# First two blocks of a fused attention and gated-projection kernel: token-partition loads of q and k, transposes on TensorE, and one explicit order of first steps

## The chip, the cores and the metric

The kernel runs on one core of one Trainium2 chip. The metric is device time in microseconds (us); lower is better. Five engines work beside each other and meet only at semaphores: PE (TensorE, matrix products and transposes by products), PEld (its weight loads), DVE (VectorE), ACT (ScalarE) and POOL (GpSimd). SP issues nearly all DMA transfers, in its program order. Each engine also works in its program order.

## The reference, cut to what matters

```
scores = (q_c @ k_c^T) / sqrt(64)            # chunks of 64 tokens, 8 batches, 8 heads, 576 tokens, head size 64
attn   = softmax(scores);  x = attn @ v_c    # x reshaped to (4608 tokens, 512)
y      = (sigmoid(x @ w_gate) * (x @ w_val)) @ w_out         # 512 -> 1536 -> 512
out    = act(y @ w2_in) @ w2_out                             # 512 -> 2048 -> 512
```

The weights w_gate, w_val, w_out, w2_in and w2_out are 64-bit floats and everything else is 32-bit. The change touches only the attention of the first two blocks and the first products with w_gate and w_val.

## The kernel before, in words

**Phases.** Phase one goes through 9 blocks of 512 tokens; for each it makes the attention output x and from it the gated product g, which goes to DRAM. Three later phases multiply by w_out, w2_in and w2_out. Only phase one changes.

**Slots.** A block of phase one has 24 slots, one for each 128 columns of w_gate (even slots) and w_val (odd slots), keys 0 to 23. A slot is one call of `proj`: 12 matmuls of 128x128 by 128x512, three (`three`, lines 482 to 484) for each of four 128-row parts kt of x, since each operand is split in a high and a low part. ACT takes the sigmoid of the gate (line 917) and DVE multiplies (line 920). Part kt of x comes from head pair p = kt of the attention.

**Attention.** The attention of a block runs as four head pairs p = 0 to 3, in steps with letters: t (q and k to head-dimension-on-partitions), s (scores on PE, line 336), m (row maximum and subtraction, DVE), e (exp, ACT, line 353), n (row sums and reciprocal, DVE), w (scaling, POOL, line 366), p (transposes of the scores on PE, line 372), c (copy out of PSUM, ACT, line 375), o (product with v on PE, line 384), x (high part, ACT, line 393) and l (low part, DVE). In block 0 they run before the first slot. The attention of block b + 1 is spread over the slots of block b.

**Three layouts of q and k** in `load` and `t`. V: 16 DMAs for each pair, 32 of 128-byte pieces at a time, then two DVE transposes of 32x32 blocks (line 317). M: 2 DMAs with 1 KB pieces, then plain matmuls against an identity (line 325) and an ACT copy (line 326). T: 4 DMAs with 256-byte pieces on the SBUF side, then four PE transposes (line 322) for q, four for k, each with an ACT copy (line 326). Block 0 takes M, V, M, T for its pairs; all later blocks take V. `swap` is an arrangement of the two heads' halves that V loads use from block 1 on.

**Weights of phase one.** `w_load` brings 512 KB of one key on SP's queue. `w_low` and `w_bits` (lines 113, 119 on DVE, 123 on ACT) and `w_split` (127 on DVE, 136 on ACT, 137 on POOL) turn the 64-bit words into a high and a low 32-bit part. This is needed once, during block 0.

**What sets the order.** The text LOADS gives the order of the first DMAs on SP: a digit loads q and k of that pair, a letter v, w the next key. The text ORDER gives the steps of block 0, where s, n, p and o each stand for a run of steps (sme, nw, pc, oxl) and c for pieces of weight conversion, f for filling matmuls. Everything else goes through `at(slot, priority, function)`: `emit(slot)` gives out the entries of a slot, by fraction and then priority, ahead of that slot's products. In `later_block`, `starts` are the slots at which pairs begin and `when` the offsets of the steps; q and k of a pair are loaded near the start of the pair two before. The constant NW = 4 says that key i is split at slot i - 4; its first conversion is at slot i - 5 and its load at slot i - 9.

**PSUM banks** have tags b0 to b7. In block 0 the transposes use b0, b2, b4 in turn; the scores b1, b3; the gate and value products b0, b1 and b2, b3; block 1 uses b4, b5 for scores, b6 for transposed scores, b6 and b7 for o.

```
kv_["ident"] = cp.tile([P, P], F32, name="ident")
...
begun = [-6.5, -6]
later_block(1, [5 * p for p in range(KT)], (0, 1, 1.5, 2, 3, 3, 5, 5, 6, 6.5, 7))
...
go = proj(("g", f), b, f"b{f % 2}")
```

Of the kernel before, what the change touches and what calls it, by code (L numbers as in the profile page):

```python
# [8 lines left out]
F32 = mybir.dt.float32  # L9
# [9 lines left out]

LOADS = "0w12wwa3bwcdww"
ORDER = (
    "t0 c1 t1 s0 t2 c1 n0 s1 c1 p0 c1 n1 s2 "
    "t3 n2 o0 p1 s3 o1 n3 p2 f2 c1 o2 p3 c1 c1 o3"
)


# [1 line left out]
def kernel(  # L30
# [201 lines left out]
    class Whole:  # L232
# [14 lines left out]

        def swap(self, p):

            return self.b != REST and self.how[p] == "V"  # L250

        def load(self, p):
            t = self.alloc("qk")
            how = self.how[p]
            if how == "V":

                t = t.rearrange("p i (t r) -> p i t r", r=32)
            elif how == "T":

                t = t.rearrange("p i (j h d) -> p i j h d", h=2, d=D)  # L260
            else:
                t = t.rearrange("p i (h j d) -> p i h j d", h=2, d=D)
            for i, src in enumerate((q, k)):
                if self.b == REST:
                    for g in range(4):
                        h, j = divmod(g, 2)
                        for c in range(RS // 32):
                            nc.sync.dma_start(
                                out=t[32 * g:32 * g + 32, i, c::RS // 32],
                                in_=src[:, 2 * p + h, BS + 32 * c:BS + 32 * c + 32, 32 * j:32 * j + 32].rearrange(  # L270
                                    "b i r -> i b r"
                                ),
                            )
                else:
                    rows = src[batch(self.b), 2 * p:2 * p + 2, :BS]
                    if how == "M":
                        nc.sync.dma_start(
                            out=t[:, i].rearrange("i h j d -> i h (j d)"),
                            in_=rows.rearrange("h (i j) d -> i h (j d)", j=NC),
                        )  # L280
                    elif how == "T":
                        for h in range(2):
                            nc.sync.dma_start(
                                out=t[:, i, :, h], in_=rows[h].rearrange("(i j) d -> i j d", j=NC)
                            )
                    else:
                        n = 2 if self.swap(p) else 1
                        step = BS // n
                        for u in range(n):
                            for g in range(4):  # L290
                                h, j = divmod(g, 2)
                                part = rows[h ^ u, u * step:(u + 1) * step, 32 * j:32 * j + 32]
                                nc.sync.dma_start(  # L293
                                    out=t[32 * g:32 * g + 32, i, u * step // 32:(u + 1) * step // 32],
                                    in_=part.rearrange("(t i) r -> i t r", i=32),
                                )
            self.qk[p] = t
# [14 lines left out]
        def t(self, p):  # L312
            qk, how, ident = self.qk[p], self.how[p], kv_["ident"]
            self.T[p] = t = self.alloc("qkT")
            for i in range(2):
                if how == "V":
                    nc.vector.transpose(out=t[:, i].rearrange("p (t i) -> p t i", i=32), in_=qk[:, i])
                    continue
                b = self.bank(0, [P, NC, P], "T")
                for j in range(NC):  # L320
                    if how == "T":
                        nc.tensor.transpose(b[:, j], qk[:, i, j].rearrange("p h d -> p (h d)"), ident)
                    else:
                        for h, hs in enumerate(heads):
                            nc.tensor.matmul(b[hs, j], lhsT=qk[:, i, h, j], rhs=ident, start=True, stop=True)
                nc.scalar.activation(t[:, i].rearrange("e (i j) -> e j i", j=NC), b, AF.Copy)

        def s(self, p):
            t = self.T[p]
# [75 lines left out]
    def first_block():  # L405
        ft = ps.tile([P, BS], F32, tag="b5", name="fill")

        def fill(n):
            for _ in range(n):
                nc.tensor.matmul(ft, lhsT=z[:, :P], rhs=z, start=True, stop=True)  # L410

        pieces = []
        for i in range(NW + 1):
            pieces.append((w_low, keys[i]))
            pieces.append((w_bits, keys[i]))
            if i:
                pieces.append((w_split, keys[i - 1]))
        nl = [0]

        def wl(n):  # L420
            for _ in range(n):
                w_load(keys[nl[0]])
                nl[0] += 1

        def conv(n):
            while n and pieces:
                fn, key = pieces.pop(0)
                fn(key)
                if fn is w_split and nl[0] < NW + 5:
                    wl(1)  # L430
                n -= fn is not w_low

        z = pool["sg"].tile([P, BS], F32R, tag="sg", name="z", bufs=4)
        nc.vector.memset(f32(z), 0.0)
        kv_["ident"] = cp.tile([P, P], F32, name="ident")
        make_identity(nc, kv_["ident"])
        a = Whole(
            0, [["b0", "b2", "b4"], "b1", "b3", "b6", "b7", "b5"],
            lambda nm: wp.tile([P, 2, BS], F32, tag="w", name=nm), "MVMT",
        )  # L440
        for c in LOADS:
            if c == "w":
                wl(1)
            elif c in "0123":
                a.load(int(c))
            else:
                a.v_load("abcd".index(c))
        for c in ORDER.split():
            if c[0] == "f":
                fill(int(c[1:]))  # L450
            elif c[0] == "c":
                conv(int(c[1:]))
            else:
                for fn in {"t": "t", "s": "sme", "n": "nw", "p": "pc", "o": "oxl"}[c[0]]:
                    getattr(a, fn)(int(c[1:]))
        conv(99)
        assert nl[0] == NW + 5, nl

    def block_load(a, p):
        a.load(p)  # L460

    def later_block(b, starts, when):

        bufs = {"qk": 3, "qkT": 1, "sp": 2, "vd": 2}

        def alloc(nm):
            cols = BS // 2 if nm == "vd" else BS
            return pool["u"].tile([P, 2, cols], F32, tag=nm, name=nm, bufs=bufs[nm])

        a = Whole(b, [None, "b4", "b5", "b6", "b6", "b7"], alloc, "V" * KT)  # L470
        for p, s0 in enumerate(starts):
            at(begun[-2] + 0.5, 5, a.load, p)
            begun.append(s0)
            at(s0 + 0.5, 5, a.v_load, p)
            for fn, dt in zip("tsmenwpcoxl", when):
                at(s0 + dt, {"s": 0, "p": 0, "o": 0, "m": 1, "e": 1, "c": 1, "x": 1}.get(fn, 3), getattr(a, fn), p)


    def three(o, pairs, start=True, open_=False):
        for i, (ah, al, bh, bl) in enumerate(pairs):  # L480
            first, last = start and i == 0, i == len(pairs) - 1
            nc.tensor.matmul(o, lhsT=ah, rhs=bh, start=first, stop=False, skip_group_check=open_)  # L482
            nc.tensor.matmul(o, lhsT=ah, rhs=bl, start=False, stop=False, skip_group_check=open_)  # L483
            nc.tensor.matmul(o, lhsT=al, rhs=bh, start=False, stop=last, skip_group_check=open_)  # L484

    def proj(key, b, tag):
        w = W[key]
        o = ps.tile([P, BS], F32, tag=tag, name="pr")
        kts = [slice(kt * P, (kt + 1) * P) for kt in range(KT)]
        three(o, [(w[:, 0, ks], w[:, 1, ks], X[b, kt][:, 0], X[b, kt][:, 1]) for kt, ks in enumerate(kts)])  # L490
        return o

# [308 lines left out]
        dst = gR if b == REST else gT[i // (B // 2)][i % (B // 2)]  # L803
        nc.sync.dma_start(out=dst[f * P:(f + 1) * P, :], in_=sg)

    begun = [-6.5, -6]
    later_block(1, [5 * p for p in range(KT)], (0, 1, 1.5, 2, 3, 3, 5, 5, 6, 6.5, 7))
    for b in range(2, NB):
        later_block(
            b, [NS * (b - 1) + 6 * p - 6 for p in range(KT)], (0, 2, 3, 4, 5, 5.5, 7, 7, 8, 9, 10)  # L810
        )

    NW = 4
    for i, key in enumerate(keys):
        if i >= NW + 5:
            at(i - NW - 5, 2.5, w_load, key)
        if i > NW:
            at(i - NW - 1, 6, w_low, key)
            at(i - NW - 1, 6, w_bits, key)
        if i >= NW:  # L820
            at(i - NW, 5.5, w_split, key)
    slot = 26
# [69 lines left out]
    with tc.manual_schedule():  # L892
# [18 lines left out]
        for b in range(NB):  # L911
            for f in range(F1):
                slot = NS * b + 2 * f
                emit(slot)
                go = proj(("g", f), b, f"b{f % 2}")
                sg = pool["sg"].tile([P, BS], F32, tag="sg", name="sg", bufs=4)
                nc.scalar.activation(sg, go, AF.Sigmoid)  # L917
                emit(slot + 1)
                vo = proj(("v", f), b, f"b{2 + f % 2}")
                nc.vector.tensor_tensor(out=sg, in0=vo, in1=sg, op=ALU.mult)  # L920
                at(slot + 2, 7, g_store, b, f, sg)
        emit(NS * NB)
# [42 lines left out]
```

## Time and profile before

| | before |
|---|---|
| median of 3 runs | 1678.91 us |
| lowest and highest run | 1675.12, 1679.11 us |
| the profiled execution's own time | 1678.13 us |
| its span in the trace | 1676.2 us |
| PE busy in the span | 98% |

The span runs from the first to the last profiled instruction; the execution's time is 1.93 us longer than the span. All times of rows below are counted from the start of the span.

### The profile page before, as it was taken

The page shows a single profiled execution, that of the slowest core. Times are in us where ns is not written, and L with a number is a line of the kernel's source. Part 1 is how long each engine was busy: PE and PEld are TensorE (multiplying, and loading weights), DVE is VectorE, ACT ScalarE, POOL GpSimd, SP SyncE. Part 2 cuts the span into 40 slices and gives each one's busy share as a digit, 9 for nine tenths or more (in the row PEclk, how much of TensorE's full clock was granted, in tenths as well). Part 3 has the DMA queues.
Part 4 walks back from the last instruction along what each step waited for, and adds up shares of the span by engine and source line. Part 5 has one row for each costly group of instructions (what it writes and reads, how often), then busy time and mean ns, then how long its engine had stood idle before and what let it go on. Part 6 is the DMA issues. An engine that isn't in the chain of part 4 may idle for free.

```text
span 1676.2 us, 29838 instructions
## 1 busy us (share of the span) xinstructions
PE 1640.7 (98%) x10658; PEld 1514.1 (90%) x10658; DVE 1153.0 (69%) x1841; ACT 851.1 (51%) x1558; POOL 723.3 (43%) x666
## 2 busy tenths in 40 slices
PE   5899999999999999999999999999999999999999
PEld 4678888887888888899999999999999999999998
DVE  5874455554555541287777777888787899889887
ACT  4663455444544541255555565555554555555553
POOL 2442444443444340155555564444350465545544
PEclk7999999999999999999999999999999999999999
DMA  7676777777787776535744763323427944554462
GB/s 197 158 196 170 207 197 219 224 227 211 212 243 221 191 259 241 212 120 135 229 151 151 252 229 132 151 113 143 151 114 296 354 138 113 168 151 104 124 189 39
DMA packets 408613, 307.14 MB, mean 183 GB/s; under 512 B 284688, under 2 KB 330768, under 8 KB 408464
## 3 DMA queue, kind: packets, MB, share of 16 engines
q1 hardware_dynamic: 405264, 304.84, 59.1%
q8 instruction: 84, 1.38, 0.3%
q10 hardware_dynamic: 3200, 0.39, 0.1%
q14 instruction: 65, 0.53, 0.1%
HBM read 179.83 MB, written 125.30 MB: 182 GB/s over the span
## 4 chain that ended last, share of the span: by engine, by line
PE 87%; DVE 4%; SPq 4%; DMA 3%; issue 1%; ACT 1%; POOL 0%; DVEq 0%; ACTq 0%; POOLq 0%
PE P L483 18%; PE P L484 18%; PE P L482 18%; PE pr L482 10%; PE pr L484 10%; PE pr L483 10%; SPq L293 2%; DMA raw<-in_moe_w_gate_dram 1%; DVE z L515 1%; PE O L384 1%; PE S L336 1%; PE PT L372 1%; SPq L310 1%; DVE z L526 1%; DMA vd<-in_v_dram 1%
## 5 line engine op out<-in xcount | busy, mean ns | idle before, releaser
L483 PE MATMUL P<-z,w 128*128 128x384 f32 x1344 | 450.4, 335 | 1.6 <-POOL z L526 0.8
L482 PE MATMUL P<-z,w 128*128 128x384 f32 x1344 | 449.0, 334 | 0.0
L484 PE MATMUL P<-z,w 128*128 128x384 f32 x1344 | 449.0, 334 | 0.0
L526 POOL TENSOR_TENSOR z<-z 128x384 fp32r<-128x384 f32 x256 | 291.2, 1149 | 361.2 <-ACT z L519 355.1
L482 PE MATMUL pr<-x,w 128*128 128x512 f32 x864 | 345.6, 400 | 0.0
L484 PE MATMUL pr<-x,w 128*128 128x512 f32 x864 | 339.4, 393 | 0.0
L483 PE MATMUL pr<-x,w 128*128 128x512 f32 x864 | 338.8, 392 | 0.0
L519 ACT ACTIVATE z<-z 128x384 fp32r<-128x384 f32 x420 | 211.4, 522 | 165.4 <-DVE z L515 73.5
L920 DVE TENSOR_TENSOR sg<-pr,sg 128x512 f32<-128x512 f32 x108 | 74.5, 690 | 289.4 <-PE pr L484 120.1
L483 PEld LDWEIGHTS P<-z,w 128*128 128x128 f32 x1344 | 252.3, 188 | 4.7 <-POOL z L526 2.6
L484 PEld LDWEIGHTS P<-z,w 128*128 128x128 f32 x1344 | 252.3, 188 | 0.0
L482 PEld LDWEIGHTS P<-z,w 128*128 128x128 f32 x1344 | 252.3, 188 | 0.0
L526 POOL TENSOR_TENSOR op<-in,op 128x384 fp32r<-128x384 f32 x126 | 142.4, 1135 | 196.7 <-ACT op L519 195.7
L484 PEld LDWEIGHTS pr<-x,w 128*128 128x128 f32 x864 | 163.4, 189 | 35.2
L482 PEld LDWEIGHTS pr<-x,w 128*128 128x128 f32 x864 | 163.5, 189 | 34.6
L483 PEld LDWEIGHTS pr<-x,w 128*128 128x128 f32 x864 | 163.7, 189 | 32.6
L519 ACT ACTIVATE op<-in 128x384 fp32r<-128x384 f32 x252 | 128.5, 524 | 111.3 <-DVE in L515 54.2
L515 DVE TENSOR_TENSOR z<-z 128x384 f32<-128x384 f32 x198 | 179.4, 933 | 4.0 <-POOL z L526 4.0
L917 ACT ACTIVATE sg<-pr 128x512 f32<-128x512 f32 x108 | 64.5, 597 | 223.4 <-PE pr L484 217.8
L484 PE MATMUL P<-op,w 128*128 128x384 f32 x504 | 168.3, 334 | 0.0
L482 PE MATMUL P<-op,w 128*128 128x384 f32 x504 | 168.3, 334 | 0.0
L483 PE MATMUL P<-op,w 128*128 128x384 f32 x504 | 168.3, 334 | 0.0
(64 smaller groups left out, 2186.5 us busy)
## 6 DMA issues: line engine op xcount, KB each, us to landing
uT<-ua SPq DMA_DIRECT2D x96, 384.0 KB, 2.3
z<-uT SPq DMA_DIRECT2D x96, 384.0 KB, 6.0
gT<-sg SPq DMA_DIRECT2D x96, 256.0 KB, 4.6
in<-gT SPq DMA_DIRECT2D x48, 384.0 KB, 4.2
raw<-in_moe_w_out_dram SPq DMA_DIRECT2D x28, 512.0 KB, 5.7
w<-swi SPq DMA_DIRECT2D x28, 512.0 KB, 5.6
w<-swp SPq DMA_DIRECT2D x28, 512.0 KB, 7.2
swi<-st SPq DMA_DIRECT2D x24, 512.0 KB, 5.0
```

The lines of the kernel that those rows point to most:

```text
L293: nc.sync.dma_start(out=t[32 * g:32 * g + 32, i, u * step // 32:(u + 1) * step // 32], in_=part.rearrange("(t i) r -> i t r", i=32),)
L310: nc.sync.dma_start(out=t[:, :, hs], in_=rows.rearrange("(g k) d -> k g d", k=P))
L336: nc.tensor.matmul(banks[h ^ u][hs, c], lhsT=t[rows, 0, ts], rhs=t[rows, 1, ts], start=True, stop=True)
L372: nc.tensor.transpose(b[:, cs], self.SP[p][:, 0, cs], kv_["ident"])
L482: nc.tensor.matmul(o, lhsT=ah, rhs=bh, start=first, stop=False, skip_group_check=open_)
L483: nc.tensor.matmul(o, lhsT=ah, rhs=bl, start=False, stop=False, skip_group_check=open_)
L484: nc.tensor.matmul(o, lhsT=al, rhs=bh, start=False, stop=last, skip_group_check=open_)
L515: (eng or nc.vector).tensor_tensor(out=op_src(p, key), in0=x, in1=y, op=ALU.subtract)
L519: nc.scalar.activation(o[:, 0], op_src(p, key), AF.Copy)
L526: eng.tensor_tensor(out=o[:, 1], in0=op_src(p, key), in1=f32(o[:, 0]), op=ALU.subtract)
L917: nc.scalar.activation(sg, go, AF.Sigmoid)
L920: nc.vector.tensor_tensor(out=sg, in0=vo, in1=sg, op=ALU.mult)
```

## The change

The first block's pairs take the layouts M, M, T, T. The second block's pairs take S, V, S, S, where S is T with the `swap` arrangement (8 DMAs for a pair; two DVE transposes are replaced by eight PE transposes and two ACT copies). T and S put token j * 128 + i on partition i, so that each DRAM piece is 256 bytes, and the ACT copy needs no rearrangement. LOADS and ORDER are new; ORDER names every step by its own letter, with A for the first conversion of a key, B for its split, L for a weight load and k for one part (three matmuls) of a product. `proj` is cut in parts (`proj_part`), so that the value product's parts 0 and 1 and the gate product's part 0 run before the last pairs are done. The filling matmuls go. Key i is now split at slot i - 2, its first conversion is at slot i - 3 and its load at slot i - 8. The starts and offsets of block 1 are new.

```
-LOADS = "0w12wwa3bwcdww"
+LAYOUT = "MMTT"
+LOADS = "10www23wabcd"
 ORDER = (
-    "t0 c1 t1 s0 t2 c1 n0 s1 c1 p0 c1 n1 s2 "
-    "t3 n2 o0 p1 s3 o1 n3 p2 f2 c1 o2 p3 c1 c1 o3"
+    "t1 t0 A0 A1 s0 A2 B0 t2 s1 m0 e0 t3 n0 w0 p0 m1 e1 c0 s2 B1 n1 w1 m2 o0 L L s3 x0 p1 "
+    "l0 e2 k01 c1 n2 o1 m3 x1 e3 w2 p2 l1 c2 L n3 w3 k11 o2 x2 k00 l2 p3 c3 o3 L x3 A3 l3 "
 )
...
-                    elif how == "T":
-                        for h in range(2):
-                            nc.sync.dma_start(
-                                out=t[:, i, :, h], in_=rows[h].rearrange("(i j) d -> i j d", j=NC)
-                            )
+                    elif how in "TS":
+                        n = 2 if self.swap(p) else 1
+                        for u in range(n):
+                            js = slice(u * NC // n, (u + 1) * NC // n)
+                            for h in range(2):
+                                nc.sync.dma_start(
+                                    out=t[:, i, js, h],
+                                    in_=rows[h ^ u].rearrange("(j i) d -> i j d", i=P)[:, js],
+                                )
...
-            0, [["b0", "b2", "b4"], "b1", "b3", "b6", "b7", "b5"],
-            lambda nm: wp.tile([P, 2, BS], F32, tag="w", name=nm), "MVMT",
+            0, [["b1", "b3"], "b4", "b5", "b6", "b6", "b7"],
+            lambda nm: wp.tile([P, 2, BS], F32, tag="w", name=nm), LAYOUT,
...
-        a = Whole(b, [None, "b4", "b5", "b6", "b6", "b7"], alloc, "V" * KT)
+        a = Whole(b, [["b4", "b5"], "b4", "b5", "b6", "b6", "b7"], alloc, how)
...
+    def proj_part(key, b, kt):
+        w, ks = W[key], slice(kt * P, (kt + 1) * P)
...
+        args = w[:, 0, ks], w[:, 1, ks], X[b, kt][:, 0], X[b, kt][:, 1]
+        three(o[0], [args], start=kt == 0, stop=kt == KT - 1, open_=True)
+
+    def proj(key, b):
+        for kt in range(parts.get((key, b), (None, 0))[1], KT):
+            proj_part(key, b, kt)
+        return parts.pop((key, b))[0]
...
-    begun = [-6.5, -6]
-    later_block(1, [5 * p for p in range(KT)], (0, 1, 1.5, 2, 3, 3, 5, 5, 6, 6.5, 7))
+    begun = [-5.5, -2.5]
+    later_block(1, [3.0, 8, 13.0, 17.0], (-1.5, 1.5, 2.0, 2.0, 2.5, 3.0, 5.0, 5, 6.0, 7.0, 7.0), "SVSS")
...
-    NW = 4
+    NA, NW, NL = 4, 2, 8
     for i, key in enumerate(keys):
-        if i >= NW + 5:
-            at(i - NW - 5, 2.5, w_load, key)
-        if i > NW:
-            at(i - NW - 1, 6, w_low, key)
-            at(i - NW - 1, 6, w_bits, key)
+        if i >= NL:
+            at(i - NL, 2.5, w_load, key)
+        if i >= NA:
+            at(i - NW - 1, 7, w_low, key)
+            at(i - NW - 1, 7, w_bits, key)
         if i >= NW:
             at(i - NW, 5.5, w_split, key)
```

## Rows read from the trace of the kernel before

**Rows 1.** The profile page's first part: busy time of each engine.
```profile
PE 1640.7 (98%) x10658; PEld 1514.1 (90%) x10658; DVE 1153.0 (69%) x1841; ACT 851.1 (51%) x1558; POOL 723.3 (43%) x666
```

**Rows 2.** Busy time by stretch: stretch, length, engines' busy time (count), clock, DMA share, GB/s.
```profile
0.00:39.10 39.10, 22.11 (x346) 18.53 (x346) 20.36 (x50) 17.59 (x28) 7.84 (x12) 0.72 0.80 207
39.10:51.90 12.80, 10.62 (x61) 8.04 (x58) 8.47 (x16) 6.76 (x12) 4.43 (x4) 0.67 0.39 63
51.90:89.10 37.20, 32.57 (x256) 26.08 (x256) 32.32 (x56) 23.36 (x36) 16.98 (x13) 0.95 0.77 210
89.10:129.20 40.10, 37.01 (x282) 29.74 (x281) 29.25 (x58) 25.39 (x39) 15.45 (x12) 1.00 0.67 171
129.20:201.70 72.50, 72.50 (x561) 59.39 (x560) 35.09 (x74) 32.31 (x51) 20.91 (x23) 1.00 0.66 185
```

**Rows 3.** Timeline of PE: start us, us, engine, line, operation, [idle before <-releaser].
```profile
39.11 0.79 PE L482 MATMUL pr<-x,w 128*128 128x512 f32 x1
...
40.13 0.63 PE L484 MATMUL pr<-x,w 128*128 128x512 f32 x1
...
40.56 0.63 PE L482 MATMUL pr<-x,w 128*128 128x512 f32 x1
...
47.28 0.52 PE L482 MATMUL pr<-x,w 128*128 128x512 f32 x1
...
51.72 0.40 PE L482 MATMUL pr<-x,w 128*128 128x512 f32 x1
...
83.57 0.69 PE L384 MATMUL O<-sp,vd 64*64 64x64 f32 x32 [2.79 <-ACT sp L375]
...
126.47 0.39 PE L482 MATMUL pr<-x,w 128*128 128x512 f32 x1
...
129.19 0.39 PE L482 MATMUL pr<-x,w 128*128 128x512 f32 x1
```

**Rows 4.** The chain of waits in order of time, two pieces eighteen microseconds apart.
```profile
135.28 0.62 PE O L384 x32
...
153.42 0.62 PE O L384 x32
```

**Rows 5.** Timeline of SP's queue in the first 30 us: start us, time to issue.
```profile
7.96 3.90 SPq L293 DMA_DIRECT2D qk<-in_k_dram  x8
...
23.31 3.53 SPq L310 DMA_DIRECT2D vd<-in_v_dram  x4
```

**Rows 6.** Timeline of all engines: steps of block 0, one of block 1.
```profile
3.62 3.44 PE L325 MATMUL T<-ident,qk 128*64 128x128 f32 x32 [3.62 <-DMA qk<-in_q_dram]
...
18.43 1.13 PE L336 MATMUL S<-qkT 64*64 64x64 f32 x32
...
18.54 1.13 ACT L326 ACTIVATE qkT<-T 128x512 f32<-128x512 f32 x1 [0.63 <-PE T L325]
...
25.14 1.97 PE L322 MATMUL T<-ident,qk 128*128 128x128 f32 x8
...
27.04 0.72 PE L384 MATMUL O<-sp,vd 64*64 64x64 f32 x32
...
31.94 0.63 ACT L353 ACTIVATE sp<-sp 128x512 f32<-128x512 f32 x1 [1.72 <-DVE sp L348]
...
38.05 1.14 PE L384 MATMUL O<-sp,vd 64*64 64x64 f32 x32 [0.69 <-ACT sp L375]
...
97.29 0.60 PE L372 MATMUL PT<-ident,sp 128*128 128x128 f32 x4
```

**Rows 7.** Instruction groups of the first 130 us: count, busy us, mean ns, idle before.
```profile
L123 ACT ACTIVATE raw<-raw 128x512 f32<-128x512 f32 x24 | 16.3, 679 | 18.0 <-DVE raw L119 14.4 <-DMA qk<-in_k_dram 2.2 <-issue 1.2
...
L317 DVE STREAM_TRANSPOSE qkT<-qk 128x512 f32<-128x512 f32 x12 | 8.0, 695 | 6.5 <-DMA qk<-in_k_dram 3.4 <-DMA qk<-in_q_dram 3.2
```

**Rows 8.** Timelines of DVE and POOL late in block 0.
```profile
103.91 0.43 DVE L113 TENSOR_SCALAR raw<-raw 128x512 int32<-128x512 uint32 x1 [2.65 <-DMA raw<-in_moe_w_gate_dram]
...
119.80 1.29 POOL L137 TENSOR_TENSOR w<-raw,w 128x512 fp32r<-128x512 f32 x1 [2.11 <-ACT w L136]
```

More of the change, by code (lines that the diff above doesn't have):

```diff
@@ L248, in swap @@
         def swap(self, p):
-            return self.b != REST and self.how[p] == "V"
+            return self.b != REST and self.how[p] in "VS"
         def load(self, p):
@@ L280, in load @@
                         )
-                    elif how == "T":
-                        for h in range(2):
-                            nc.sync.dma_start(
-                                out=t[:, i, :, h], in_=rows[h].rearrange("(i j) d -> i j d", j=NC)
-                            )
+                    elif how in "TS":
+                        n = 2 if self.swap(p) else 1
[6 more added lines that the diff above has]
+                                )
                     else:
@@ L320, in t @@
                 for j in range(NC):
-                    if how == "T":
+                    if how in "TS":
                         nc.tensor.transpose(b[:, j], qk[:, i, j].rearrange("p h d -> p (h d)"), ident)
@@ L325, in t @@
                             nc.tensor.matmul(b[hs, j], lhsT=qk[:, i, h, j], rhs=ident, start=True, stop=True)
-                nc.scalar.activation(t[:, i].rearrange("e (i j) -> e j i", j=NC), b, AF.Copy)
+                dst = t[:, i].rearrange("e (i j) -> e j i", j=NC) if how == "M" else t[:, i]
+                nc.scalar.activation(dst, b, AF.Copy)
         def s(self, p):
@@ L410, in fill, with wl @@
                 nc.tensor.matmul(ft, lhsT=z[:, :P], rhs=z, start=True, stop=True)
[L412 to L417, printed above, removed]
-        nl = [0]
[L420 to L431, printed above, removed]
+        nl = [0]
+        def wl():
+            w_load(keys[nl[0]])
+            nl[0] += 1
         z = pool["sg"].tile([P, BS], F32R, tag="sg", name="z", bufs=4)
@@ L442, in first_block @@
             if c == "w":
-                wl(1)
+                wl()
             elif c in "0123":
@@ L448, in first_block, with later_block @@
         for c in ORDER.split():
+            n = int(c[1:] or 0)
             if c[0] == "f":
-                fill(int(c[1:]))
-            elif c[0] == "c":
-                conv(int(c[1:]))
-            else:
[L454 to L457, printed above, removed]
+                fill(n)
+            elif c[0] == "L":
+                wl()
+            elif c[0] == "A":
+                w_low(keys[n])
+                w_bits(keys[n])
+            elif c[0] == "B":
+                w_split(keys[n])
+            elif c[0] == "k":
+                proj_part(keys[n % 10], 0, n // 10)
+            else:
+                getattr(a, c[0])(n)
+        assert nl[0] == NL, nl
     def block_load(a, p):
         a.load(p)
-    def later_block(b, starts, when):
+    def later_block(b, starts, when, how="V" * KT):
         bufs = {"qk": 3, "qkT": 1, "sp": 2, "vd": 2}
@@ L474, in later_block, with three @@
             at(s0 + 0.5, 5, a.v_load, p)
+            first = {"s": 0, "p": 0, "o": 0, "m": 1, "e": 1, "c": 1, "x": 1, "t": 3 if how[p] == "V" else 0}
             for fn, dt in zip("tsmenwpcoxl", when):
-                at(s0 + dt, {"s": 0, "p": 0, "o": 0, "m": 1, "e": 1, "c": 1, "x": 1}.get(fn, 3), getattr(a, fn), p)
-    def three(o, pairs, start=True, open_=False):
+                at(s0 + dt, first.get(fn, 3), getattr(a, fn), p)
+    def three(o, pairs, start=True, open_=False, stop=True):
         for i, (ah, al, bh, bl) in enumerate(pairs):
@@ L483, in three @@
             nc.tensor.matmul(o, lhsT=ah, rhs=bl, start=False, stop=False, skip_group_check=open_)
[L484 to L491, printed above, removed]
+            nc.tensor.matmul(o, lhsT=al, rhs=bh, start=False, stop=stop and last, skip_group_check=open_)
+    parts = {}
+    def proj_part(key, b, kt):
+        w, ks = W[key], slice(kt * P, (kt + 1) * P)
+        if kt == 0:
+            kind, f = key
+            tag = f"b{f % 2}" if kind == "g" else f"b{2 + f % 2}"
+            parts[key, b] = [ps.tile([P, BS], F32, tag=tag, name="pr"), 0]
+        o = parts[key, b]
+        assert o[1] == kt
+        o[1] = kt + 1
+        args = w[:, 0, ks], w[:, 1, ks], X[b, kt][:, 0], X[b, kt][:, 1]
[4 more added lines that the diff above has]
+        return parts.pop((key, b))[0]
     turn = [0]
@@ L914 @@
                 emit(slot)
-                go = proj(("g", f), b, f"b{f % 2}")
+                go = proj(("g", f), b)
                 sg = pool["sg"].tile([P, BS], F32, tag="sg", name="sg", bufs=4)
@@ L918 @@
                 emit(slot + 1)
-                vo = proj(("v", f), b, f"b{2 + f % 2}")
+                vo = proj(("v", f), b)
                 nc.vector.tensor_tensor(out=sg, in0=vo, in1=sg, op=ALU.mult)
```

## The prediction

> **What bounds the kernel now.** I read the page's busy shares first: PE is busy 98% of the span [rows 1], so a change of order can win only where PE idles or runs at a low clock. The second view is busy time by stretch, cut near the starts of slots 0, 2, 12, 24 and 48 [rows 2]. PE idles 17.0 us before slot 0 (39.1 less 22.11), 2.2 us in slots 0 and 1, 4.6 and 3.1 us in the rest of block 0, and nothing in the next 72.5 us. The granted clock is 0.72 of full ahead of slot 0 and 0.67 in slots 0 and 1; it is 1.00 from 89 us on. So all that can be won lies before 129.2 us, where slot 24 (block 1) starts [rows 3]. Whatever moves that start moves the end by as much, since PE is full behind it [rows 2].
>
> The third view is PE's timeline [rows 3]. Slot 0 starts at 39.11, slot 1 at 47.28, slot 2 at 51.72, slot 24 at 129.19. A slot whose operands are there takes 2.72 us (126.47 to 129.19, 0.227 per matmul); slot 0's matmuls are 0.43 us apart (40.13 to 40.56), which is 1.2 GHz against 2.4. In steady state six slots with one pair's attention take 18.14 us [rows 4], 1.8 more than 6 x 2.72 = 16.3. So slots 2 to 23 need 22 x 2.72 = 59.8 and 4 x 1.8 = 7.2, together 67.0, and took 77.5: 10.4 us are stalls and low clock. The 2.79 us wait of o for ACT at 83.57 is the largest single one shown [rows 3].
>
> **What is late there.** SP issues the 8 DMAs of one V-layout tensor in 3.90 us, 16 for a pair in twice that [rows 5], and anything queued behind, weights above all, waits. One result: DVE stood 2.65 us waiting for a key's raw words at 101.3 to 103.9 [rows 8]. DVE is busy 61.6 of the 77.3 us from 51.9 to 129.2 [rows 2], in strict order, so one late operand delays all that stands behind it.
>
> **The change, part by part.** The sum follows the start of slot 24 in five legs.
>
> 1. *First pairs.* Block 0's second load was a V pair; now it is M, two DMAs. Pair 1's first tensor is loaded at the same place as pair 0's before, so transposes start at 3.62 again. Two M pairs take 2 x 3.44 us on PE [rows 6], to 10.5; the last ACT copy 1.1 more, to 11.6. The scores (1.13) end at 12.8, while ACT works through what is queued ahead of pair 0's exp: four weight activations of 0.68 [rows 7] and the two copies of pair 2 (1.1 each [rows 6]), 4.9 us, to 16.5. Here m waits on DVE behind three conversions, which are over by then.
> 2. *Exp to o.* For pair 3 before, exp started at 31.94 and its o at 38.05, 6.1 us later [rows 6]. So o of pair 0 starts at about 22.6, against 27.04 before for the first o [rows 6]. The loads must keep up: q, k, four keys and v are 5 MB, at the stretch's mean of 207 GB/s [rows 2] 25 us for the last byte, v of pair 3; the last v was issued by 26.8 before [rows 5]. They are no limit, because o of pair 3 comes later.
> 3. *Pairs 1 to 3.* The four o's started from 27.04 to 38.05, 11.0 us [rows 6]. The three early product parts add nine matmuls on PE, 9 x 0.43 = 3.9 us if none falls into a gap, 0 if all do. On POOL pair 1's scaling now stands behind key 1's low part, 1.3 us [rows 8]; that is inside these ends. I take half: o of pair 3 starts at 22.6 + 11.0 + 2.0 = 35.6 and ends at 36.7.
> 4. *Slots 0 and 1.* 24 - 9 = 15 matmuls are left, and the transposes of block 1's pair 0. At 1.2 GHz that is 15 x 0.43 + 1.97 (eight transposes at 25.14 [rows 6]) = 8.4; at 2.4 GHz 15 x 0.227 + 2 x 0.60 (four transposes at 97.29 [rows 6]) = 4.6. I take the middle, 6.5: 43.2. Before, slot 2 started at 51.7. Slot 1 no longer waits for DVE's transposes of a V pair; the data is asked for right behind the last weight load, with 4 us instead of 7.8 on SP. Pair 1's V load behind it still takes 7.8 and holds up key 8's load, which is first needed at slot 5.
> 5. *Slots 2 to 23.* 67.0 us as above, and 2 x 1.2 = 2.4 for the transposes of pairs 2 and 3, which are new on PE: 69.4. So without stalls slot 24 starts at 112.6.
>
> **Stalls left** can't be read directly: the ends are none and the old 10.4. For fewer: three pairs cost SP half, DVE loses six transposes of 0.70 us [rows 7], and loads of weights lie five slots ahead of their first use instead of four. For as many: keys are split two slots ahead, not four. The last key's split ended at 121.1 [rows 8], 5.4 us before slot 23 [rows 3]; two slots later (2 x 18.14 / 6 = 6.0 us) it would be 0.7 late, and more conversions fall into the slots. ACT gains six copies of 1.1 us; it was busy 48.8 of 77.3 us [rows 2], so the copies hide, but only as long as the order lets them. I take 5 us, the middle: slot 24 at 117.6, 11.6 us earlier.
>
> **The rest costs nothing**: leaving out the two filling matmuls and the letters' order on idle engines is covered by waits, and block 2's first loads, moved to slots 13.5 and 17.5, still stand four slots before use. If that cover went, DVE's transposes of those pairs would stand in front of the rest as at 103.9, some 2.7 us. From block 1 on nothing else moves.
>
> So 1678.1 - 11.6 = **1666.5 us**, from the profiled execution's own time, which is 0.8 below the median of the runs shown.
>
> **A rule weighed.** The transposes of block 0's last pairs and three pairs of block 1 go through PE. The row: at 97.29 four such transposes took 0.60 us within a stretch of granted clock 1.00 [rows 2, 6], and no fall followed. The Trainium skill, page "TensorE: Matmul & The Clock Gate", section "Part 4: PE-mode transpose", says that such transposes don't count as busy in the way matmuls do and don't bring the full clock. By that rule slots 0 and 1 and the new transposes would stay at 1.2 GHz; by the trace they need not once products surround them. No row shows transposes alone at length.
>
> **The rivals.**
>
> *DVE and the conversions set the pace.* The lead of two slots is too short, PE waits for POOL's low parts, and the 10.4 us of stalls stay. For it: the 0.7 us worked out above and DVE at 80%. Against it: DVE loses 6 x 0.70 = 4.2 us. Slot 24 then starts at 112.6 + 10.4 = 123.0, and the time is 1672.
>
> *The clock stays low.* The clock is 1.2 GHz through slots 0 and 1 (1.9 us above my middle), and around each of the two later transposed pairs one slot runs at 1.2 GHz (2 x 2.7) beside 2 x 0.8 for the transposes: 8.9 us more, 1675. For it: 0.67 in slots 0 and 1 [rows 2]. Against it: 1.00 with transposes in every block after that. It is what the rule of the Trainium skill named above would bring.
>
> *The loads do not come earlier.* 256-byte pieces move no faster than the V loads, block 0 ends as late as before, and PE only carries the added transposes (3 x 1.2 = 3.6) while the 2.2 us that it idles in slots 0 and 1 [rows 2] are saved: 1679.5, no change. For it: SP needed 3.53 us for four v loads of such pieces [rows 5], 0.9 each against the usual 0.5. Against it: M replaces V where block 0 waited.
>
> *Slower.* Block 1's transposes and scores now share banks b4 and b5, and PE meets them in order: each of three transposed pairs waits for DVE's m of the pair before, each of four score steps for ACT's copies. The price is bounded by PE's 2.79 us wait for ACT [rows 3]: 7 x 2.79 = 19.5, so slot 24 starts at 117.6 + 19.5 = 137.1 and the time is 1686. From 11.6 / 7 = 1.7 us for each meeting it decides the sign. Against it: t stands three slots ahead of s, two more than m needs; only pair 3's t falls into the slot of pair 2's m.
>
> **How the numbers follow.** The forecast has 0.60, the conversions' pace 0.18, the low clock 0.06, loads no earlier 0.08, the shared banks 0.08. About 0.3%, 5 us, is what a measurement of this kernel can tell from no change. Faster by more: the forecast, and 0.15 of the 0.24 of the next two, 0.75. Within: their other 0.09 and loads no earlier, 0.17. Slower: the banks, 0.08. The forecast's own range: at best legs 3 and 4 are 2.0 and 1.9 shorter and no stall is left, 8.9 less, 1658; at worst they are as much longer and the stalls 10.4, 1676. I keep 1658 and cut the other end to 1675, which still takes in the two middle rivals and leaves out some 0.2.
>
> **What would show it.** Right: the last o of block 0 starting near 35.6 instead of 38.05; slot 1 over before 45 with no wait on DVE; slot 24's first product near 117.6; SP with 8 short DMAs for a pair; PE full behind it, as before. Wrong: products waiting for POOL's line 137 (the conversions' pace); half-rate slots after transposes (clock); a first o no earlier than 27 (loads); PE waiting at t and s on DVE or ACT (banks). A changed length of blocks 1 to 8 would be outside all of these.

## The result, and the profile after

The changed kernel takes 1662.35 us (median of 4 runs, 1661.29 to 1662.72) against 1677.01 for the kernel before beside it (4 runs, 1674.72 to 1679.11): ratio 0.9912, 95% interval 0.9894 to 0.9930. The forecast was 1666.5, range 1658 to 1675. The profiled execution took 1662.72 us with a span of 1660.9, 15.3 less span than before.

First the busy shares of the page, as in [rows 1], and then busy time by stretch, as in [rows 2]: stretch, its length, then busy time (count) of PE, PEld, DVE, ACT and POOL, granted clock, DMA share, GB/s. The cuts are near the starts of slots 0, 2, 12, 24 and 48 of the changed kernel, and the last row is block 4, slots 96 to 119.

```profile
PE 1637.8 (99%) x10688; PEld 1511.6 (91%) x10688; DVE 1154.3 (69%) x1833; ACT 852.4 (51%) x1566; POOL 720.7 (43%) x666
```

```profile
0.00:31.40 31.40, 20.92 (x361) 17.00 (x361) 17.81 (x47) 17.36 (x28) 7.41 (x12) 0.95 0.99 249
31.40:35.90 4.50, 4.50 (x32) 3.77 (x25) 3.89 (x6) 3.72 (x7) 1.30 (x1) 1.00 0.36 63
35.90:68.00 32.10, 31.20 (x230) 25.18 (x229) 28.93 (x52) 22.90 (x36) 14.95 (x11) 1.00 0.83 238
68.00:110.60 42.60, 39.85 (x357) 31.80 (x356) 36.02 (x65) 31.45 (x49) 18.92 (x15) 1.00 0.68 175
110.60:183.20 72.60, 72.60 (x562) 59.43 (x562) 35.76 (x76) 33.11 (x54) 21.65 (x24) 1.00 0.68 188
...
330.10:408.80 78.70, 75.42 (x561) 61.64 (x560) 37.22 (x75) 36.13 (x58) 32.10 (x34) 0.96 0.77 227
```

Against [rows 2], the clock ahead of slot 0 is 0.95 of full (0.72 before), what is left of slots 0 and 1 (15 of their 24 matmuls and eight transposes) takes 4.5 us without any idle time (12.6 before, for all 24, at 0.67), and PE idles 3.7 us in the rest of block 0 (7.7 before). DMA moves 249 GB/s ahead of slot 0 instead of 207. Block 4 is the exception: PE idles 3.3 us there and the clock is 0.96.

PE's timeline, the rows that answer to [rows 3, 6]: start us, us, engine, line, operation, [idle before <-releaser].

```profile
20.50 0.27 PE L390 MATMUL O<-sp,vd 64*64 64x64 f32 x1
...
30.82 0.69 PE L390 MATMUL O<-sp,vd 64*64 64x64 f32 x32 [0.69 <-ACT sp L381]
31.44 0.50 PE L480 MATMUL pr<-x,w 128*128 128x512 f32 x1
...
33.62 1.04 PE L327 MATMUL T<-ident,qk 128*128 128x128 f32 x8
35.88 0.40 PE L480 MATMUL pr<-x,w 128*128 128x512 f32 x1
...
75.89 0.69 PE L390 MATMUL O<-sp,vd 64*64 64x64 f32 x32 [1.90 <-ACT sp L381]
80.84 1.06 PE L327 MATMUL T<-ident,qk 128*128 128x128 f32 x8 [0.84 <-PE pr L482]
...
110.65 0.39 PE L480 MATMUL pr<-x,w 128*128 128x512 f32 x1
```

The first o starts at 20.50 (27.04 before), the last of block 0 at 30.82 (38.05), slot 2 at 35.88 (51.72) and slot 24 at 110.65 (129.19). So 18.5 us are won where block 1's slots start, but only 15.3 arrive at the end. Where the other 3 went is the subject of the last three experiments.

SP's queue in the first 30 us (answers to [rows 5]) and two ACT copies of transposes, the first from an M pair, the second from a T pair (answers to [rows 6]):

```profile
2.26 0.47 SPq L278 DMA_DIRECT2D qk<-in_k_dram  x1
2.77 0.47 SPq L105 DMA_DIRECT2D raw<-in_moe_w_gate_dram  x1
...
15.06 4.93 SPq L315 DMA_DIRECT2D vd<-in_v_dram  x8
...
22.47 3.17 SPq L287 DMA_DIRECT2D qk<-in_q_dram  x4
25.69 5.14 SPq L287 DMA_DIRECT2D qk<-in_k_dram  x4
```

```profile
9.34 1.11 ACT L332 ACTIVATE qkT<-T 128x512 f32<-128x512 f32 x1 [0.19 <-PE T L330]
...
14.28 0.58 ACT L332 ACTIVATE qkT<-T 128x512 f32<-128x512 f32 x1
```

The first two pairs are asked for within 2.8 us; all of v is issued by 20.0 (26.8 before). The copy of a T pair takes half of an M pair's. It writes its destination in order; in the kernel before, where the T pair's copies still rearranged, two of them took 1.99 us (at 27.25). The last two rows of SP's queue are pair 0 of block 1 in S: 8.3 us for eight DMAs, so an issue has no fixed price. M's took 0.45 to 0.47 each, these about 1.0.

### The profile page after: what moved, and what is told of

It is laid out like the page before. It is cut to its first block, busy times and chain, and to the rows that moved or that the text cites. A ratio compares the mean times of both kernels' runs of the same rounds, so it can differ in the third digit from the quotient of the medians.

```text
span 1660.9 us, 29856 instructions
## 1 busy us (share of the span) xinstructions
PE 1637.8 (99%) x10688; PEld 1511.6 (91%) x10688; DVE 1154.3 (69%) x1833; ACT 852.4 (51%) x1566; POOL 720.7 (43%) x666
## 4 chain that ended last, share of the span: by engine, by line
PE 91%; DVE 4%; ACT 1%; SPq 1%; issue 1%; DMA 1%; POOL 0%; DVEq 0%; POOLq 0%; ACTq 0%
PE P L481 18%; PE P L482 18%; PE P L480 18%; PE pr L480 11%; PE pr L482 11%; PE pr L481 11%; PE O L390 1%; DVE z L525 1%; PE S L342 1%; PE PT L378 1%; DVE raw L128 1%; DVE z L536 1%; SPq L298 0%; DVE raw L120 0%; DMA gR<-sg 0%
## 5 line engine op out<-in xcount | busy, mean ns | idle before, releaser
L480 PEld LDWEIGHTS pr<-x,w 128*128 128x128 f32 x864 | 162.7, 188 | 34.1
```

## The experiments

**Which part brings it.** Four kernels, compared at the starts of slots 2 and 24 and in time. e1 has the new order, leads and starts with the old layouts; e2 the new layouts alone; e3 and e4 undo one block's layouts each.

e1:
```
-LAYOUT = "MMTT"
-LOADS = "10www23wabcd"
+LAYOUT = "MVMT"
+LOADS = "01www23wabcd"
...
-    "t1 t0 A0 A1 s0 ..."
+    "t0 t1 A0 A1 s0 ..."
...
-    later_block(1, ..., "SVSS")
+    later_block(1, ..., "VVVV")
```

> The new order, early product parts, short leads and starts of the changed kernel, with block 0's pairs laid out M, V, M, T as before and all of block 1 in V. Theory A (the gain is the freed SP queue and the transposes taken off DVE, so it needs the layouts): the second pair again waits for 16 DMAs on SP, o of pair 3 starts near 36 instead of 30.8, block 1's transposes stand on DVE again, slot 24 starts at 121 or later (before 129.2, changed kernel 110.7) and the time is about 1673. Rival B (the written order and the early product parts do it, the layouts hardly matter): slot 24 at 113 or earlier, 1665 or less.

e2, on the kernel before (with the changed `swap`, `load`, `t` and the priority of t):
```
-            ... "MVMT",
+            ... "MMTT",
...
-        a = Whole(b, [None, "b4", "b5", "b6", "b6", "b7"], alloc, "V" * KT)
+        a = Whole(b, [["b4", "b5"], "b4", "b5", "b6", "b6", "b7"], alloc, how)
...
-    later_block(1, [5 * p for p in range(KT)], (0, 1, 1.5, 2, 3, 3, 5, 5, 6, 6.5, 7))
+    later_block(1, [5 * p for p in range(KT)], (0, 1, 1.5, 2, 3, 3, 5, 5, 6, 6.5, 7), "SVSS")
```

> The kernel before with the new layouts alone (M, M, T, T and S, V, S, S); its own order of loads and steps, leads and starts stay. Theory A (the layouts carry most): the V loads leave SP's queue in the first 10 us, o of pair 3 starts near 33, slot 24 starts near 119 and the time is about 1667. Rival B (the order does it): PE's added transposes, 3 x 1.06 us, cost as much as they save, slot 24 at 126 or later, 1674 or more.

e3 has e1's edits but for the last, e4 only the last.

> The changed kernel with block 0's pairs M, V, M, T again; block 1 keeps S, V, S, S. Theory A: 16 DMAs of 0.49 us on SP come back ahead of everything else, the loads behind them move by 6 to 7 us, o of pair 3 starts at 35 to 37 and slot 24 moves by as much: 1667 to 1669. Rival B: block 0 is bound by its chain of engines and not by its loads, so less than 2 us: 1664.

> The changed kernel with block 1 in V throughout; block 0 keeps M, M, T, T. Slot 2 should start at 35.9 in any case. Theory A (SP's queue and DVE were what stalled block 0's slots): DVE gets back 6 transposes of 0.65 us and SP 24 DMAs of 0.49 us, PE loses 3 x 1.06 us of transposes; slots 2 to 23 take 78 to 80 us instead of 74.8 and the time is 1665 to 1667. Rival B (the added PE transposes are dead weight): slots 2 to 23 take 72 us and the time is 1659.

Measured (slot starts from each kernel's timeline of PE; time: median of 4 runs, ratio to the kernel before on the same chip with its 95% interval):

| kernel | slot 2 | slot 24 | us | ratio |
|---|---|---|---|---|
| before | 51.7 | 129.2 | | |
| e1, order alone | 42.4 | 120.5 | 1670.6 | 0.9949 (0.9930 to 0.9968) |
| e2, layouts alone | 44.4 | 117.6 | 1668.4 | 0.9935 (0.9914 to 0.9956) |
| e3, block 0's layouts undone | 43.6 | 118.3 | 1667.7 | 0.9932 (0.9914 to 0.9950) |
| e4, block 1's layouts undone | 34.1 | 117.9 | 1668.1 | 0.9933 (0.9913 to 0.9954) |
| changed kernel | 35.9 | 110.7 | 1662.35 | 0.9912 (0.9894 to 0.9930) |

Slot 24 starts in e1, e2, e3 and e4, in this order, each fence one kernel's timeline of PE. Each is from one profile. The changed kernel, e7, e8 and e11 don't differ ahead of slot 24, and theirs starts at 110.65, 110.11, 111.62 and 112.70, so less than some 2.6 us there can be chance; the length of slots 2 to 23 is steadier, 74.7 to 74.8 us in all four.

```profile
120.48 0.39 PE L480 MATMUL pr<-x,w 128*128 128x512 f32 x1
```
```profile
117.55 0.39 PE L488 MATMUL pr<-x,w 128*128 128x512 f32 x1
```
```profile
118.34 0.39 PE L480 MATMUL pr<-x,w 128*128 128x512 f32 x1
```
```profile
117.87 0.39 PE L480 MATMUL pr<-x,w 128*128 128x512 f32 x1
```

At slot 24 the order is worth 8.7 us alone and the layouts 11.6; together they bring 18.5, which can't be told from the sum, 20.3. Neither rival B of e1 nor that of e2 holds: both halves matter. Theory A of e1 misses too: slot 24 starts just ahead of 121, though o of pair 3 is later than put (38.20, not 36), and the time is 2.4 us below 1673, so the order alone does more than it allowed. e2 comes out near what its theory A has (o of pair 3 at 32.89). Block 0's layouts are worth 7.7 us (e3), all of it ahead of slot 2; o of pair 3 starts at 38.51, even later than the 35 to 37 put, and the time falls into the range of theory A. SP's queue of e1 shows it: the V pair's first tensor takes SP 3.9 us and the second as long again, and the first weight goes out at 9.65 instead of 2.77.

```profile
1.75 3.91 SPq L298 DMA_DIRECT2D qk<-in_q_dram  x8
5.71 3.90 SPq L298 DMA_DIRECT2D qk<-in_k_dram  x8
9.65 0.45 SPq L105 DMA_DIRECT2D raw<-in_moe_w_gate_dram  x1
```

Block 1's layouts are worth 7.2 us at slot 24 (e4), all of it behind slot 2, where e4 is even 1.8 us earlier: 0.9 because PE has no transposes in slot 1, and 0.9 that it is ahead from the first early part on. Slots 2 to 23 take 83.8 us in e4 against 74.8, more than the 78 to 80 expected, and the time, 1668.1, lies above theory A's 1667. So three pairs' transposes, 1.06 us each on PE, buy 9 us in the slots. What grows is PE's wait for converted weights: 4.3 us for POOL's low parts and 2.4 for ACT's high part, against 0.4 in all in the changed kernel. The longest of them in e4's timeline of PE:

```profile
70.82 0.50 PE L480 MATMUL pr<-x,w 128*128 128x512 f32 x1 [2.40 <-ACT w L137]
```

SP takes 10.2 to 13.6 us for the 16 DMAs of each of these three pairs in e4 and 6.5 to 8.3 for the 8 DMAs in S, and DVE has six transposes more. e4 changes both loads at once, and which of the two holds it up more is not separated.

The two blocks' layouts also need each other. Beside block 0's old layouts, block 1's shorten slots 2 to 23 by only 3.3 us (78.1 in e1, 74.8 in e3) and bring 2.1 at slot 24. Without block 1's, block 0's bring 2.6 there instead of 7.7 (e1 to e4). These two differences at slot 24 are within chance; the lengths are not: slots 2 to 23 take 5.7 us more in e4 than in e1, so most of the earlier start is lost again there.

**The early product parts.** e5 leaves out k01, k11 and k00; e9 puts filling matmuls (zeros times zeros, result not used) in their places.

e5:
```
-    "l0 e2 k01 c1 n2 o1 m3 x1 e3 w2 p2 l1 c2 L n3 w3 k11 o2 x2 k00 l2 p3 c3 o3 L x3 A3 l3 "
+    "l0 e2 c1 n2 o1 m3 x1 e3 w2 p2 l1 c2 L n3 w3 o2 x2 l2 p3 c3 o3 L x3 A3 l3 "
```

> The changed kernel without the three early product parts (k01, k11, k00): slots 0 and 1 run whole, behind block 0's attention. Theory A (the early parts fill waits of PE and keep its clock up): o of pair 3 starts no earlier than at 30 instead of 30.8, slot 2 starts 2 to 4 us later than 35.9, and if the clock falls again in the gaps, at 40; the time is 1664 to 1666. Rival B (they only stand in front of o on PE): o of pair 3 starts 2 us earlier, slot 2 starts at about 36, 1662.

e9, with the bank of the filling matmuls set to b0:
```
+    "l0 e2 f3 c1 n2 o1 m3 x1 e3 w2 p2 l1 c2 L n3 w3 f3 o2 x2 f3 l2 p3 c3 o3 L x3 A3 l3 "
```

> The changed kernel without its three early product parts, but with three filling matmuls of zeros (same shape, same place on PE, result unused) in place of each. Tells what the early parts are worth as work done early and what as activity that keeps PE's clock up; without both, slot 2 started at 41.0 instead of 35.9. Theory C (the clock is most of it): no half-rate stretch between 26 and 37 us, slot 2 at 35.9 + 9 x 0.23 = 38, 1664.5. Rival W (the work is most of it): the clock falls all the same or matters little, slot 2 at 40 to 41, 1667.

Slot 2 starts at 41.03 in e5 and at 37.96 in e9, against 35.88. The two rows, e5 first:

```profile
41.03 0.39 PE L480 MATMUL pr<-x,w 128*128 128x512 f32 x1
```
```profile
37.96 0.39 PE L480 MATMUL pr<-x,w 128*128 128x512 f32 x1
```

Busy time from 26.6 to 36.8 us, e5 first, then e9, then the changed kernel:

```profile
26.60:36.80 10.20, 7.79 (x81) 5.92 (x79) 6.29 (x13) 5.06 (x9) 2.34 (x2) 0.50 0.61 149
```
```profile
26.60:36.80 10.20, 9.38 (x105) 7.25 (x105) 6.89 (x14) 6.52 (x13) 2.54 (x3) 1.00 0.60 132
```
```profile
26.60:36.80 10.20, 9.37 (x105) 7.22 (x105) 7.53 (x15) 6.51 (x13) 2.51 (x3) 1.00 0.62 138
```

Without the parts PE is given 1.2 GHz for the whole stretch; with fillings in the same places, 2.4 GHz. Ahead of that stretch, from 23.2 to 26.6 us, all three were granted 2.4 GHz, and PE was busy 1.68 us in e5 and 2.36 in the other two. Of the 5.15 us that the parts are worth at slot 2, 3.07 are the clock (41.03 to 37.96) and 2.08 the nine matmuls (9 x 0.23 = 2.07). Theory C holds. The sum closes on one profile of each kernel, but the three agree up to the parts: the first o starts at 20.26 in e5, 20.54 in e9 and 20.50. Rival B of e5 falls: without the parts, o of pair 3 starts no earlier (31.55 against 30.82). The times follow less sharply: 1667.7 for e5, above theory A's 1666, ratio 0.9928 (0.9910 to 0.9947), and 1663.4 for e9, ratio 0.9908 (0.9891 to 0.9925). The intervals overlap with the changed kernel's, so the split is shown at slot 2 and not in the time.

**The lead of the conversions.** e6 splits keys three slots ahead instead of two.

```
-    ... p3 c3 o3 L x3 A3 l3 "
+    ... p3 c3 o3 L L x3 A3 B2 A4 l3 "
...
-    NA, NW, NL = 4, 2, 8
+    NA, NW, NL = 5, 3, 9
```

> The changed kernel with keys split three slots ahead instead of two (the split of key 2 and the first conversion of key 4 move ahead of slot 0, loads one slot earlier too). Theory A (two slots are enough, since PE waits for POOL's low part only 0.4 us in all): slots 2 to 23 stay at 74 to 76 us and the time at 1661 to 1664. Rival B (the conversions set the pace of block 0): 2 to 4 us less, 1658 to 1660.

Slot 2 starts at 36.61 and slot 24 at 111.02, 74.41 us apart against 74.77. The time, 1661.8, ratio 0.9894 (0.9875 to 0.9914), can't be told from the changed kernel's. Theory A holds and rival B falls. The short lead costs next to nothing.

**Block 1's last V pair.** e10 lays out all four pairs of block 1 in S ("SSSS").

> The changed kernel with block 1's pair 1 in S as well. Theory A (V loads on SP and DVE's transposes cost more than PE's): PE gains 1.06 us, DVE loses 1.3 and SP 8 DMAs; slots 2 to 23 take 72 to 74 us instead of 74.8, 1660 to 1662. Rival B (the one V pair was left because SP or DVE have room there): 76 us, 1663 to 1664.

Slots 2 to 23 take 76.6 us (35.41 to 112.05), 1.9 more, and the time is 1662.7, ratio 0.9899 (0.9883 to 0.9916): no gain, as rival B has it. But this does not show that a pair is better left to DVE. Behind a wait of o (1.86 us, before 76.16) e10's clock falls, and eight matmuls run at half rate:

```profile
75.00:80.00 5.00, 3.84 (x71) 3.20 (x72) 4.54 (x8) 3.18 (x6) 2.30 (x3) 0.74 0.74 175
```

They cost some 1.6 us, by an estimate of 0.2 us for each, which is most of the 1.9. The changed kernel has the same wait (1.90 us, before 75.89) and keeps 1.00. Whether the layout or chance brought the fall is open.

**Where 3 us went again.** The chain before block 4's o at 375.76 in the changed kernel leads back over ACT to a late store of g. Two candidates: buffers (e7) and raw words of w2_in (`in_moe_w_in_dram` in the trace) that come late (e8, e11).

e7:
```
-  ... tag="sg", name="sg", bufs=4)
+  ... tag="sg", name="sg", bufs=5)
```

> The changed kernel with five buffers for the sigmoid's output instead of four; about the 3 us given back in block 4 (slots 96 to 119 take 78.7 us, 75.1 before the change). Theory S (the sigmoid waits for a buffer whose store stands behind 16 DMAs of a V pair on SP): the 3.3 us wait of o and the low clock behind it go, block 4 takes about 73, 1656. Rival R (DVE stands 6.4 us for raw words of w_in that were loaded late, and holds up the products): the wait of DVE stays, block 4 stays above 76, 1660 to 1662.

e8, and e11 with -2 in place of -1:
```
-            (0, w_load, a), (0, w_load, b), (4, w_low, a),
+            (-1, w_load, a), (-1, w_load, b), (4, w_low, a),
```

> The changed kernel with the raw words of w_out, w2_in and w2_out asked for one slot earlier in block 1 to 7's preparation of later weights, so ahead of a V pair's 16 DMAs where both fall together. Rival R: DVE's 6.4 us wait in block 4 goes, slots 96 to 119 take about 73 us, 1656. Theory S: the sigmoid's buffer still waits for its store, block 4 stays above 76, 1660 to 1662.

> The changed kernel with the later weights' raw words asked for two slots earlier; one slot earlier block 4 took 73.5 us instead of 78.7, but block 6 took 74.0 instead of 72.5, and the time was 1659.6. If late raw words behind V loads are all of the stalls in blocks 4 and 6, both take 72.5 to 73 us: 1656 to 1657. If loading earlier only moves the meeting of loads and stores to other slots, one of them stays above 74: 1658 to 1661.

The changed kernel's block 4, SP's queue and then DVE, and DVE of e7:

```profile
356.59 5.01 SPq L298 DMA_DIRECT2D qk<-in_q_dram  x8
361.64 3.90 SPq L298 DMA_DIRECT2D qk<-in_k_dram  x8
365.59 1.00 SPq L105 DMA_DIRECT2D raw<-in_moe_w_in_dram  x2
```
```profile
370.02 0.43 DVE L114 TENSOR_SCALAR raw<-raw 128x512 int32<-128x512 uint32 x1 [6.44 <-DMA raw<-in_moe_w_in_dram]
```
```profile
369.23 0.43 DVE L114 TENSOR_SCALAR raw<-raw 128x512 int32<-128x512 uint32 x1 [6.19 <-DMA raw<-in_moe_w_in_dram]
```

Two raw loads stand behind a V pair's 16 DMAs, which take SP 9 us, and DVE, in its program order, waits 6.4 us for them. Five buffers leave that wait, o's (3.04 us) and block 4's length (77.2 us); the time is 1663.9, ratio 0.9911 (0.9888 to 0.9935): theory S falls, though theory R's 1660 to 1662 is missed too. Asked for one slot earlier, the words keep DVE at most 1.92 us in block 4, which takes 73.5 us; the time is 1659.6, ratio 0.9882 (0.9862 to 0.9902), above the 1656 of theory R, and block 6 now takes 74.0. Two slots earlier blocks 4 and 6 both take 72.5; block 4 of e11 in the view of busy time by stretch:

```profile
332.20:404.70 72.50, 72.50 (x562) 59.38 (x560) 37.92 (x75) 35.88 (x57) 32.18 (x34) 1.00 0.80 229
```

PE no longer idles and keeps its clock. e11 takes 1656.3 us (1655.7 to 1658.4), ratio 0.9863 (0.9848 to 0.9878), an interval that lies wholly below the changed kernel's: the best version of this study. Theory R is shown. The kernel before had the same wait in its block 4:

```profile
387.78 0.43 DVE L113 TENSOR_SCALAR raw<-raw 128x512 int32<-128x512 uint32 x1 [5.65 <-DMA raw<-in_moe_w_in_dram]
```

So the change deepened a stall rather than made one. Block 4 in one profile of each kernel, four of the eleven that ask for the words at the old place and then e8 and e11:

| kernel | DVE's longest wait for the words | o's longest wait | granted clock | block 4 |
|---|---|---|---|---|
| e4 | 4.34 | 1.19 | 1.00 | 73.8 |
| before | 5.65 | 2.50 | 1.00 | 75.1 |
| changed kernel | 6.44 | 3.28 | 0.96 | 78.7 |
| e6 | 7.47 | 4.32 | 0.96 | 79.0 |
| e8 | 1.92 | 0.86 | 1.00 | 73.5 |
| e11 | none | none | 1.00 | 72.5 |

In all eleven o waits 3.13 to 3.16 us less than DVE. Where the clock stays at 1.00 (e4, e10, e1, before), block 4 is longer than e11's 72.5 by o's wait, to a tenth. In the other seven the clock is 0.96 to 0.98, and it is 1.4 to 2.9 us longer still. So of the 3.6 us that block 4 lost by the change, 0.8 are wait and the rest is clock. Why the words come later in some kernels than in others is open: the edits of e1 to e6, e9 and e10 don't touch the code of blocks 2 to 8.

## Why the prediction was right, and where it was off

The sign, the place and the range were right: but for 0.6 us in block 6, all that was won was won ahead of slot 24, by the steps that the five legs name. Legs 1 to 4 were sized 7 us too long in all, and "from block 1 on nothing else moves" was put at nothing and cost 3 us. The two errors have opposite signs, so that the time came within 4.2 us of the forecast is partly luck.

1. *First pairs.* Pair 0's exp was put at 16.5; it started at 16.03.
2. *Exp to o.* Taken as 6.1 us from pair 3 before; it took 4.5 (16.03 to 20.50). Before, DVE began the row sums 1.61 us after the exp had started, behind the l of an earlier pair; here 0.65. And p took 0.65 us on PE instead of 1.11.
3. *Pairs 1 to 3.* "I take half: o of pair 3 starts at 22.6 + 11.0 + 2.0 = 35.6" failed by 4.8 us: it started at 30.82. Of that, 0.5 is leg 1, 1.6 leg 2 and 2.7 this leg: from the first o it took 10.3 instead of 13.0. The early parts, put at 2.0, cost no time here; e5, without them, has its last o at 31.55. They kept the clock up, which the working did not think of: it priced them at 1.2 GHz.
4. *Slots 0 and 1.* 6.5 was the middle of 4.6 and 8.4; 4.4 us (31.44 to 35.88) is the end at full clock, for the same reason. "4 us instead of 7.8 on SP" was wrong: the S pair took 8.3. It cost nothing in slot 1, where PE did not wait.
5. *Slots 2 to 23.* 69.4 us and 5 of stalls; 74.8 measured, so 5.4 of stalls. The new transposes took 1.06 each, not 1.2. The middle of 0 and 10.4 was a choice, and that it came out is luck in part: without the layouts of block 1 (e4) the stretch takes 83.8, more than before the change. "Three pairs cost SP half" is too much; they cost it 3.8 to 5.2 us less each, of 10.2 to 13.6.

Together slot 24 came 7.0 us earlier than put, 110.7 against 117.6. Then block 4 lost 3.6 us, block 6 gained 0.6, and of 18.5 us 15.3 stayed. "If that cover went" named DVE waiting behind late loads, but at the wrong place: not block 2's q and k, but raw words of w2_in in block 4.

**The rivals.** The conversions' pace: fell; PE waited for POOL's low part 0.4 us in all of block 0, and a longer lead changed nothing (e6). It does come back with the V pairs (e4). The low clock: the other way, 0.95 ahead of slot 0 and 1.00 from there to slot 24. Eight transposes took 1.04 us at 33.62 in a stretch of granted clock 1.00. The Trainium skill, page "TensorE: Matmul & The Clock Gate", section "Part 4: PE-mode transpose", says that transposes don't bring the full clock; this did not decide here, where matmuls stand around them, and no run had transposes alone at length. Loads no earlier: fell, v was out 6.8 us sooner, and the first o started at 20.50. The shared banks: PE's longest wait at a t or s behind slot 2 was 0.84 us, far below the 1.7 from which they would have decided.

## What to carry to other kernels

Count DMAs on an issuing queue by their issue time, read where they stand: a V pair's 16 DMAs in front of a weight sent it out 6.9 us later (9.65 instead of 2.77). A late operand on an in-order engine shows up as a wait somewhere else, blocks later. When a start is bound by a chain over several engines, put real work that is ready into PE's gaps: it counts twice, as work and as clock. After a gain at the front, look at every later stage for one that lost again, and follow its wait back to the queue.

## What the runs showed of the hardware that was not expected

Three matmuls of 0.23 us in each of three gaps decided between 1.2 and 2.4 GHz for 10 us (granted clock 0.50 in e5, 1.00 in e9), and filling matmuls did it as well as products. An ACT copy of 128x512 from PSUM took 0.58 us with the destination in order and 1.11 us with it rearranged. One DMA of q or k took SP 0.45 us to issue at the start of the kernel and about 1.0 on the mean of an S pair's eight.
